# Batch 0 of a fused attention and feed-forward kernel: decay folded into V, one exponential per score block, weights loaded in thirds

## The chip, the cores and the metric

The kernel runs on one core of one Trainium2 chip. A core has five engines that each work through their own instructions in order: TensorE (PE, matrix products), VectorE (DVE), ScalarE (ACT), GpSimd (POOL) and SyncE (SP, which here only issues transfers). They wait for one another through semaphores. Transfers between the chip's memory and the core's on-chip memory (SBUF) go through 16 DMA engines, fed by queues that SP, ACT and POOL issue into. PE writes its results into PSUM, a small memory of banks of 128 x 512 float32, and the other engines copy from there.

The metric is the device time of one execution in microseconds (us); lower is better. The output has to agree with the reference within a tolerance.

## The reference

Causal attention with a decay, for 8 batches, 8 heads, 576 positions and head size 64, followed by an RMS norm and a SwiGLU feed-forward network (FFN) over the 4608 tokens:

```python
scores = scale * np.matmul(q, k.transpose(0, 1, 3, 2))       # q, k, v: (8, 8, 576, 64)
cum = np.cumsum(np.maximum(s, 0.0), axis=-1)                 # s: (8, 8, 576)
bias = -(cum[:, :, :, None] - cum[:, :, None, :])
scores = np.where(causal, -1000000000.0, scores + np.minimum(bias, 0.0))
scores = scores - np.max(scores, axis=-1, keepdims=True)
attn = np.exp(scores)
attn = attn / (np.sum(attn, axis=-1, keepdims=True) + 1e-09)
x = np.matmul(attn, v)           # heads side by side: (4608, 512)
...
rms = np.sqrt(np.mean(x * x, axis=-1, keepdims=True) + 1e-06)
xn = x / rms * rms_g
g = xn @ w_gate                  # (512, 1536)
silu = g * (1.0 / (1.0 + np.exp(-g)))
out = (silu * (xn @ w_val)) @ w_out
```

The weight of key position j for query position i is exp(score + cum[j] - cum[i]). The factor exp(-cum[i]) is the same for all keys of a query and cancels in the division by the sum, so a kernel needs only exp(score) times exp(cum[j] - shift), with one shift for each head and batch.

## The kernel before

**Tiles.** A batch has five blocks of positions (`NSC`), four of 128 and one of 64, the tail. Because of the decay, a key block kb matters only to the queries of blocks kb and kb + 1; a flag that is worked out during the run decides at the end whether this held, and a general path (`general`) stands ready otherwise. The score step `s_step(b, kb, g)` (L225) multiplies key block kb with up to 256 queries for the four heads of head group g into two PSUM banks, one for even and one for odd heads (L250). The exponentials follow on ACT, one instruction for each head (L274), because each takes its own per-partition bias, a column of `biasK` with cum[j] minus the shift. POOL then zeroes what lies above the diagonal (L283, `affine_select`). For the tail block, one step holds all eight heads.

`av_step(b, qb, g)` (L292) multiplies the exponentials of key blocks qb - 1 (L300) and qb (L306) with V. V lies in SBUF as `v_sb`, bf16, with a 65th column of ones for each head, whose product is the sum for the division. DVE takes the reciprocal (L313) and multiplies (L315) into `x_sb`. After the second head group the sum of squares is formed, on DVE (L325) or with `act=True` on ACT (L321, Square with an accumulator), and POOL makes the norm's factor from it (L328, L331). `x_scale` (L338, DVE) multiplies the block by that factor and by the norm's gain `g_row`, giving `xs_sb`. Transposed it becomes `xnT`, the FFN's input, by four PE transposes and a copy in batch 0 (`xt_step`, L357 and L364) and by a transposing DMA later.

q and k come as float32 (`kq32`), are cast to bf16 (`cast`, L139 on ACT, L141 on POOL or DVE), transposed by PE for two heads at a time (`t_step`, L184, evicted by L190 on DVE or L192 on ACT), and their tails together in `tail_step` (L200, copies L205 and L209).

**The FFN** (`ffn(c)`, L658) takes chunks of 512 tokens. Each of its 12 blocks has four gate matmuls (L668), a tanh on ACT (L671), four value matmuls (L677), and two multiplications on DVE (U at L680, `Ht` at L673 or L685). Four groups of 12 output matmuls follow (L690), with a copy (L695) and a store (L697) each. There are nine chunks, a batch being 1.125 chunks.

**Order.** From the second batch on a planner (`step`, L599) places the attention's work between the FFN's matmuls, slot by slot, from queues for each engine (`act_side`, `pool_side`, `dve_side`, `v_side`), and `need(c)` (L646) runs it further until a chunk's input is there. Batch 0's blocks 0 to 3 are written out by hand ahead of the first chunk (L773 to L884): loads, casts, transposes, scores, products, normalizations. Between them stand `warm(n)` calls (L593), dummy matmuls that keep PE busy; the loads of the FFN's weights (`load_w`, L700, GpSimd's queue, cast on the way), here in halves of the 1536 columns; and the first part of the range check (`check_mag`, `check_max`, L368 to L375), three DVE instructions that take the largest magnitude of q and k. The tail block of batch 0 (S(4), its products and x_scale) falls to the planner in the first chunk.

The PSUM banks are held by one pool `pp` for the whole run: four single banks F (FFN results; in the prologue also second score buffers through `pairF`), one double bank S, one AV and one T.

The decay (L705 to L720) starts with the load of s on ACT's DMA queue, ahead of everything on ACT. `decay_sums` takes max(s, 0), the running sum (`tensor_tensor_scan`) and subtracts the shift, four DVE instructions; `decay_bias` transposes the result by five matmuls and copies it to `biasK`.

Of the kernel before, what the change touches and what calls it, by code (L numbers as in the profile page):

```python
# [26 lines left out]
def kernel(  # L27
# [43 lines left out]
    pp = fast.enter_context(tc.tile_pool(name="pp", bufs=1, space=bass.MemoryType.PSUM))  # L71


# [26 lines left out]

    def psF():
        return pp.tile([128, DM], FP32, name="psF", tag="F", bufs=4)

    def psF16():
        return pp.tile([128, 8, 128], BF16, name="psF16", tag="F", bufs=4)

    def psS():
        return pp.tile([128, 2, 512], FP32, name="psS", tag="S", bufs=1)

    def psAV():  # L110
        return pp.tile([128, 512], FP32, name="psAV", tag="AV", bufs=1)

    def psAV16():
        return pp.tile([128, 8, 128], BF16, name="psAV16", tag="AV", bufs=1)

    def psT():
        return pp.tile([128, 8, 128], BF16, name="psT", tag="T", bufs=1)

    def psT32():
        return pp.tile([128, 512], FP32, name="psT32", tag="T", bufs=1)  # L120
# [58 lines left out]

    def t_step(b, hp, w, pT=None, dve=None):  # L180
# [44 lines left out]
    def s_step(b, kb, g, pair=None):  # L225
# [6 lines left out]
        if pair is None:  # L232
            ps = psS()
            pair = (ps[:, 0, :], ps[:, 1, :])
# [26 lines left out]
        def exps(part):  # L261
            for h, par, o in part:
# [29 lines left out]
    def av_step(b, qb, g, ps=None, act=False):  # L292
# [3 lines left out]
        for j in range(4):  # L296
            h = 4 * g + j
            o = ps[:, j * NV:(j + 1) * NV]
            if qb > 0:
                nc.tensor.matmul(o, lhsT=E[:, eslot[b, qb - 1, g], j, 128:256],  # L300
                                 rhs=v_sb[:, p, qb - 1, h, :], start=(j == 0), stop=False)
            if qb < 4:
                d = E[:, eslot[b, qb, g], j, 0:128]
            else:
                d = E[:, eslot[b, 4, 0]].rearrange("p h (a n) -> p (h a) n", n=128)[:, h, :]
# [177 lines left out]
    def after_av(b):  # L483
        if b + 2 < B:
            (early if b else later)(v_side, 6 if b else 16, [
                lambda r=r: load_v(b + 2, r) for r in range(NSC)]
                + [lambda: done.__setitem__(("V", b + 2), slot[0])])
# [16 lines left out]
    def do_s(key, pair=None):  # L504
        b, kb, g = key
        second = s_step(b, kb, g, pair)
# [193 lines left out]
    def load_w(src, dst, i):  # L700
        fs = slice(i * (DF // 2), (i + 1) * (DF // 2))
# [13 lines left out]
    def decay_bias():  # L715
# [4 lines left out]
        nc.vector.tensor_copy(out=biasK, in_=ps[:, 0:NSC * BH].rearrange("p (a e) -> p a e", e=BH))  # L720
# [50 lines left out]
    with tc.manual_schedule():  # L771

        nc.scalar.dma_start(out=s_sb, in_=s.rearrange("b h s -> (b h) s"))  # L773
# [6 lines left out]
        nc.sync.dma_start(out=g_row, in_=moe_rms_g.rearrange("(o d) -> o d", o=1).to_broadcast([128, DM]))  # L780
        make_identity(nc, ident_bf)
        make_identity(nc, ident_f)
        nc.gpsimd.memset(v_sb[:, :, :, :, 64:65], 1.0)
# [3 lines left out]
        nc.vector.memset(stat, 0.0)  # L787
        nc.vector.memset(ss_all, 0.0)
        nc.vector.memset(acc, 0.0)
        nc.vector.memset(v_sb[64:128, :, 4, :, 0:64], 0.0)  # L790
        nc.vector.memset(kqTn[:, :, :, :, 576:640], 0.0)

# [10 lines left out]
        def pairF():  # L803
            return (psF(), psF())

        def s_first(kb, g, pair=None):
            do_s((0, kb, g), pair)()

        for w in (0, 1):
            piece(w, 0, 0, ACT)  # L810
            piece(w, 0, 1, ACT)
            piece(w, 0, 2, POOL)
            piece(w, 0, 3, POOL)
        load_v(0, 0)
        load_v(0, 1)
        load_v(0, 2)
        load_w(moe_w_gate, wg_sb, 0)
# [281 lines left out]
```

## Time and profile before

| | |
|---|---|
| time, median of 3 runs | 376.12 us (375.98 to 376.18) |
| the profiled execution's own time | 375.92 us |
| its span (first to last instruction) | 374.2 us |
| first FFN matmul | 32.12 us |
| first matmul of the second chunk | 76.35 us |
| exponentials (L274) | 352 instructions, 114.9 us on ACT |
| masks (L283) | 72 instructions, 52.2 us on POOL |
| FFN matmuls (L668, L677, L690) | 432 each, 379 ns each |
| bytes moved | 46.22 MB, 124 GB/s on average |

Busy shares are of the span. The time of the run is 1.7 us longer than the span, which begins with the first recorded instruction and ends with the last. A group's line gives its count, its busy time and the mean of one, then the idle time of its engine just ahead of it and what ended most of that. "Granted clock" is the TensorE clock that the throttle allowed; it was 1.00 in the prologue and 0.998 over the span. In the timeline's lines the columns are the start in us, the duration in us, the engine, the line, the operation, what it writes and reads, the shape, and in brackets the wait just before it with what ended it; several equal instructions in a row are drawn together with "x8". In the table by stretch, the columns after the stretch are its length, then for PE, PE's weight loads, DVE, ACT and POOL the busy us and in brackets the instructions, then the granted clock, the DMA share and GB/s.

In the trace of before, s landed at 6.24 us, the first half of k and q at 6.41 and 7.64, the second at 9.12 and 10.92, their tails at 11.8 and 12.96, and `g_row` at 13.55. The first three blocks of V landed from 14.5 to 16.4, the first half of the gate weights at 19.7 and of the value weights at 25.3, the second halves at 37.2 and 41.5.

### The profile page before, as it was taken

To read this page: it belongs to the slowest core of one execution; us is meant where nothing else is said; L and a number is where in the kernel's file an instruction comes from. 1 tells how busy PE (TensorE), PEld (TensorE's weight loads), DVE (VectorE), ACT (ScalarE), POOL (GpSimd) and SP (SyncE) were. 2 spreads that over 40 slices of the span, in tenths; PEclk is the share of its full clock that TensorE was granted. 3 is DMA by queue.
4 is the path that set the end of the run, shared out by engine and by line. 5 is a ranking of instruction groups with operands and counts; after the bars stand their busy time and mean duration, and the time that the engine had idled before them with its cause. 6 is when DMAs were issued, how large, how long until landed. Compare 5 with 4: busy or idle time off the path is not lost. (4 is left out here: it accounts for less than half of the span.)

```text
span 374.2 us, 6937 instructions
## 1 busy us (share of the span) xinstructions
PE 347.0 (93%) x2356; PEld 161.4 (43%) x2356; DVE 279.7 (75%) x525; ACT 239.8 (64%) x626; POOL 174.4 (47%) x277
## 2 busy tenths in 40 slices
PE   1867899899999999899999999999999999999993
PEld 1443444454444444344444444444444444444441
DVE  6758988589887878788889897785488548837830
ACT  3777787547877597786777776777677744323321
POOL 5865734974846575779756825522322310000000
PEclk9999999999999999999999999999999999999999
DMA  8999999899997599959999997992210230020012
GB/s 230 189 227 237 146 196 220 123 204 225 155 168 105 53 195 165 159 55 204 149 162 225 136 107 152 120 67 44 96 26 14 44 105 3 0 84 31 0 44 76
DMA packets 125626, 46.22 MB, mean 124 GB/s; under 512 B 104912, under 2 KB 120784, under 8 KB 125584
## 3 DMA queue, kind: packets, MB, share of 16 engines
q0 software_dynamic: 59920, 11.80, 42.7%
q1 hardware_dynamic: 53040, 24.33, 34.6%
q10 hardware_dynamic: 12624, 9.59, 10.5%
q8 instruction: 20, 0.33, 0.4%
q14 instruction: 22, 0.18, 0.2%
HBM read 38.16 MB, written 9.44 MB: 127 GB/s over the span
## 5 line engine op out<-in xcount | busy, mean ns | idle before, releaser
L274 ACT ACTIVATE E<-psS,biasK 128x256 bf16<-128x256 f32 (+3 forms) x352 | 114.9, 415 | 19.7 <-PE psS L250 18.1
L668 PE MATMUL psF<-xnT,wg_sb 128*128 128x512 bf16 x432 | 111.1, 379 | 2.4 <-DMA xnT<-xs_sb 1.3
L677 PE MATMUL psF<-xnT,wv_sb 128*128 128x512 bf16 x432 | 111.1, 379 | 0.1
L690 PE MATMUL psF<-wout_sb,Ht 128*128 128x512 bf16 x432 | 102.3, 379 | 0.0
L283 POOL TENSOR_SCALAR_AFFINE_SELECT E<-E 128x512 bf16<-128x512 bf16 x72 | 52.2, 725 | 93.7 <-ACT E L274 92.8
L671 ACT ACTIVATE T<-psF 128x512 f32<-128x512 f32 x108 | 64.3, 597 | 42.1 <-PE psF L668 38.7
L680 DVE SCALAR_TENSOR_TENSOR U<-T,psF 128x512 bf16<-128x512 f32 x108 | 73.6, 682 | 21.9 <-ACT T L671 21.8
L673 DVE TENSOR_TENSOR Ht<-U,psF 128x512 bf16<-128x512 bf16 x99 | 67.7, 684 | 7.5 <-PE psS L250 0.5
L668 PEld LDWEIGHTS <-wg_sb 128*128 128x128 bf16 x432 | 38.7, 98 | 46.9 <-issue 8.0
L677 PEld LDWEIGHTS <-wv_sb 128*128 128x128 bf16 x432 | 38.6, 98 | 42.8 <-issue 4.6
L690 PEld LDWEIGHTS <-Ht 128*128 128x128 bf16 x432 | 38.7, 98 | 42.1 <-issue 2.3
L338 DVE SCALAR_TENSOR_TENSOR xs_sb<-x_sb,al_all,g_row 128x512 bf16<-128x512 bf16 (+1 forms) x40 | 32.8, 822 | 16.1 <-POOL al_all L331 14.5
L695 ACT ACTIVATE osb<-psF 128x512 f32<-128x512 f32 x36 | 21.4, 595 | 33.7 <-PE psF L690 29.4
L321 ACT ACTIVATE xs_sb<-x_sb 128x512 bf16<-128x512 bf16 (+1 forms) x36 | 22.9, 639 | 22.3 <-DVE x_sb L315 22.2
L175 POOL DMA_DIRECT2D v_sb<-in_v_dram x40 | 35.3, 883 | 0.4 <-issue 0.3
L375 DVE TENSOR_TENSOR acc<-acc,mag 128x1280 bf16<-128x1280 bf16 x32 | 29.4, 936 | 0.4
L250 PE MATMUL psS<-kqT 64*128 64x256 bf16 (+2 forms) x304 | 26.8, 262 | 1.6 <-ACT E L274 1.5
L306 PEld LDWEIGHTS <-E 128*128 128x128 bf16 x320 | 22.3, 99 | 13.3 <-POOL E L283 3.4
L328 POOL TENSOR_SCALAR al_all<-ss_all 128x1 f32<-128x1 f32 (+1 forms) x40 | 11.1, 277 | 28.5 <-ACT xs_sb L321 23.0
L300 PEld LDWEIGHTS <-E 128*128 128x128 bf16 x256 | 20.6, 99 | 7.9 <-DVE x_sb L315 0.6
L331 POOL TENSOR_TENSOR al_all<-al_all,mhalf 128x1 f32<-128x1 f32 (+1 forms) x40 | 22.2, 556 | 3.3
L250 PEld LDWEIGHTS <-kqT 64*128 64x128 bf16 x320 | 10.4, 97 | 29.9 <-issue 28.6
(94 smaller groups left out, 278.8 us busy)
## 6 DMA issues: line engine op xcount, KB each, us to landing
out_dram<-osb SPq DMA_DIRECT2D x36, 256.0 KB, 2.3
kq<-in_q_dram ACTq DMA_DIRECT2D x6, 1024.0 KB, 9.5
v_sb<-in_v_dram POOLq DMA_DIRECT2D x32, 128.0 KB, 7.2
kq<-in_k_dram ACTq DMA_DIRECT2D x2, 1024.0 KB, 10.6
kqn<-in_k_dram POOLq DMA_DIRECT2D x16, 128.0 KB, 5.6
wg_sb<-in_moe_w_gate_dram POOLq DMA_DIRECT2D x2, 768.0 KB, 7.3
wv_sb<-in_moe_w_val_dram POOLq DMA_DIRECT2D x2, 768.0 KB, 10.3
wout_sb<-in_moe_w_out_dram POOLq DMA_DIRECT2D x1, 1536.0 KB, 14.1
```

The source lines that it names most:

```text
L175: nc.gpsimd.dma_start(out=v_sb[0:n, b % 2, c, :, 0:64], in_=v[b, :, c * 128:c * 128 + n, :].rearrange("h p d -> p h d"))
L250: nc.tensor.matmul(pair[par][:, j * W:j * W + M], lhsT=kT, rhs=qT, start=(j == 0), stop=(j == nj - 1))
L274: nc.scalar.activation(out=eo, in_=ei, func=AF.Exp, scale=0.125, bias=biasK[:, kb, bh:bh + 1])
L283: nc.gpsimd.affine_select(out=Ev[:, :, 0:nq], in_=Ev[:, :, 0:nq], pattern=[[0, nh], [1, nq]], compare_op=ALU.is_ge, fill=0.0, base=0, chan ...
L338: nc.vector.scalar_tensor_tensor(out=xs_sb[0:n, (b * NSC + qb) % NX, :], in0=x_sb[0:n, (b * NSC + qb) % NX, :], scalar=al_all[0:n, col:col ...
L375: nc.vector.tensor_tensor(out=acc[:, sl], in0=acc[:, sl], in1=mag[:, sl], op=ALU.max)
L668: nc.tensor.matmul(Gp, lhsT=wg_sb[:, cc, fs], rhs=xnT[:, cc, x0:x0 + DM], start=(cc == 0), stop=(cc == CC - 1))
L671: nc.scalar.activation(out=T, in_=Gp, func=AF.Tanh, scale=0.5)
L673: nc.vector.tensor_tensor(out=Ht[:, fb - 1, :], in0=pend[0], in1=pend[1], op=ALU.mult)
L677: nc.tensor.matmul(Vp, lhsT=wv_sb[:, cc, fs], rhs=xnT[:, cc, x0:x0 + DM], start=(cc == 0), stop=(cc == CC - 1))
L680: nc.vector.scalar_tensor_tensor(out=U, in0=T, scalar=1.0, in1=Gp, op0=ALU.add, op1=ALU.mult)
L690: nc.tensor.matmul(Op, lhsT=Ht[:, fb, tb * 128:(tb + 1) * 128], rhs=wout_sb[:, fb, :], start=(fb == 0), stop=(fb == FB - 1))
```

## The change

It rewrites batch 0's prologue; what the planner does with the later batches stays as it is, but for two entries in the first chunk.

- **Decay in V.** For batch 0 the factor exp(cum[j] - shift) is no longer a bias of the exponentials but multiplies V's rows. ACT writes it straight into V's 65th column (one exponential of the transposed sums), so that the column's product is still the sum for the division. V of batch 0 is loaded as float32 into `v32`, which shares a buffer with `Ht`, on GpSimd's queue, and DVE multiplies it by the column (`weigh`), one instruction for each block. After batch 0 the column is set back to ones.
- **One exponential for four heads.** Without a bias, the exponentials of a score block become one instruction (128 x 1024 elements for blocks 0 to 2, 128 x 4 x 192 for block 3, 128 x 8 x 64 for the tail). It writes the heads in the order of the two banks, and `e_head` tells the products where a head lies.
- **Head.** s goes first on SP's queue, ahead of k and q. `decay_sums` is the first work of DVE after its memsets; the memsets of `stat`, `ss_all`, `acc` and of V's tail go to POOL. Third and fourth casts of the first half of q and k, and both tails' casts, go from POOL to DVE; some evictions change between ACT and DVE.
- **Order.** Two score buffers (S) from a pool of the prologue's own (`pq`: S 2, F 2, A 1, T 1), so that the next block's scores are issued ahead of the exponential of the one before; then `pp` is opened as it was before, for the FFN. All four sums of squares are on ACT (`act=True`), that of block 0 stands ahead of the exponential of S(3,1). Batch 1's q and k loads are issued earlier. The warm-up matmuls are 6 instead of 13.
- **Weights** come in thirds, the last third issued at the end of the prologue: two more DMAs on GpSimd's queue. 
- **Check.** The three check instructions for batch 0's q leave the prologue's end and are queued for the first chunk, together with the multiplication for V's tail (`weigh(DVE, 4)`, the third entry of DVE's queue).

```diff
+    v32 = mp.tile([128, NSC, H, D], FP32, name="v32", tag="Ht", bufs=2)
...
+    def load_v0(c):
+        n = rows(c)
+        nc.gpsimd.dma_start(
+            out=v32[0:n, c], in_=v[0, :, c * 128:c * 128 + n, :].rearrange("h p d -> p h d"))
+
+    def weigh(eng, c):
+        n = rows(c)
+        eng.tensor_tensor(
+            out=v_sb[0:n, 0, c, :, 0:D], in0=v32[0:n, c],
+            in1=v_sb[0:n, 0, c, :, D:NV].to_broadcast([n, H, D]), op=ALU.mult)
...
         def exps(part):
+            if b == 0:
+
+                if part[0][1] == 0 and part[0][0] == heads[0][0]:
+                    eo = Ev.rearrange("k (a j) n -> k a j n", a=2)[:, :, :, 0:N]
+                    ei = both.rearrange("k a (j n) -> k a j n", n=W)[:, :, 0:nj, 0:N]
+                    nc.scalar.activation(out=eo, in_=ei, func=AF.Exp, scale=0.125)
+                return
...
     def after_av(b):
         if b + 2 < B:
+            def ones():
+                nc.gpsimd.memset(v_sb[:, 0, :, :, D:NV], 1.0)
+                load_v(b + 2, 0)
...
     def load_w(src, dst, i):
-        fs = slice(i * (DF // 2), (i + 1) * (DF // 2))
+        fs = slice(i * (DF // 3), (i + 1) * (DF // 3))
...
-        nc.scalar.dma_start(out=s_sb, in_=s.rearrange("b h s -> (b h) s"))
+        turn = psum("pq", (2, 2, 1, 1))
+        nc.sync.dma_start(out=s_sb, in_=s.rearrange("b h s -> (b h) s"))
...
+        nc.gpsimd.memset(stat, 0.0)
+        nc.gpsimd.memset(ss_all, 0.0)
+        nc.gpsimd.memset(acc, 0.0)
...
+        decay_sums()
...
+        bias = decay_turn()
+        ACT.activation(out=v_sb[:, 0, :, :, D], in_=bias[:, :, 0:H], func=AF.Exp)
         for w in (0, 1):
+            for r in range(4):
+                piece(w, 0, r, (ACT, ACT, DVE, DVE)[r])
+        DVE.tensor_copy(out=biasK, in_=bias)
...
+        for w in (0, 1):
+            cast(DVE, 0, w, 4, 5)
+        s00 = do_s((0, 0, 0))
+        s10 = do_s((0, 1, 0))
         do_t((0, 2, 0), pT=psT(), dve=True)
         do_t((0, 3, 0), pT=psF16(), dve=True)
+        s00()
+        load_v0(3)
+        load_w(moe_w_gate, wg_sb, 0)
+        do_t((0, 2, 1), pT=psT(), dve=False)
+        do_t((0, 3, 1), pT=psF16(), dve=True)
+        s20 = do_s((0, 2, 0))
+        s10()
...
+            load_kq(nc.sync, 1, w)
...
+        s01 = do_s((0, 0, 1))
+        load_w(moe_w_val, wv_sb, 0)
+        s20()
+        s11 = do_s((0, 1, 1))
         tail_step(0)
         done["T", 0] = 0
+        s01()
+        weigh(DVE, 0)
+        weigh(DVE, 1)
+        do_av((0, 0, 0))
+        s21 = do_s((0, 2, 1))
+        s11()
+        load_v0(4)
+        do_av((0, 1, 0), psT32())
+        weigh(DVE, 2)
         s30 = do_s((0, 3, 0))
+        s21()
+        do_av((0, 0, 1), act=True)
+        s31 = do_s((0, 3, 1))
+        s30()
+        weigh(DVE, 3)
+        s31()
+        do_av((0, 2, 0), psT32())
         do_av((0, 1, 1), act=True)
+        do_av((0, 3, 0), psT32())
         x_scale(0, 0)
+        do_av((0, 2, 1), act=True)
+        do_xt((0, 0), psF16())
         warm(2)
+        x_scale(0, 1)
         do_av((0, 3, 1), psT32(), act=True)
         load_w(moe_w_gate, wg_sb, 1)
         load_w(moe_w_val, wv_sb, 1)
         do_xt((0, 1), psF16())
         warm(2)
         x_scale(0, 2)
...
         warm(2)
         x_scale(0, 3)
         do_xt((0, 3), psF16())
-        check_mag(0, 1)
-        check_max(0)
-        check_max(1)
-        done["check", 0, 1] = 0
+        load_w(moe_w_gate, wg_sb, 2)
+        load_w(moe_w_val, wv_sb, 2)
+        turn.close()
+        turn = psum("pp", (1, 4, 1, 1))
...
-        check(0, (0,))
+        check(0)
+        later(dve_side, 4, [lambda: weigh(DVE, 4)])
+        dve_side.insert(2, dve_side.pop())
```

The second argument of `psum` gives the number of buffers for the tags S, F, A and T. A call such as `s00 = do_s(...)` issues the score matmuls and the exponential; `s00()`, called later, issues the mask.

More of the change, by code (lines that the diff above doesn't have):

```diff
@@ L825 @@
[L825 to L831 removed]
+        for r in range(4):
+            piece(0, 1, r, (ACT, ACT, DVE, POOL)[r])
+        load_v0(0)
+        load_v0(1)
+        load_v0(2)
+        for r in range(4):
+            piece(1, 1, r, DVE)
+        for w in (0, 1):
+            cast(DVE, 0, w, 4, 5)
+        s00 = do_s((0, 0, 0))
+        s10 = do_s((0, 1, 0))
```

115 lines of the change are left out of this document (37 added, 78 removed).

## The prediction

> **What bounds the kernel now.** I read the engines' shares first, then the busy time by stretch, then the timeline of the first 33 us, then what TensorE (PE) waits for afterwards.
>
> ```profile
> PE 347.0 (93%) x2356; PEld 161.4 (43%) x2356; DVE 279.7 (75%) x525; ACT 239.8 (64%) x626; POOL 174.4 (47%) x277
> ```
>
> ```profile
> 10.40:20.00 9.60, 7.58 (x66) 4.79 (x65) 6.90 (x17) 7.53 (x22) 7.78 (x11) 1.00 1.80 180
> 20.00:24.00 4.00, 2.49 (x40) 1.80 (x38) 2.84 (x13) 3.62 (x12) 2.59 (x5) 1.00 1.21 194
> 24.00:28.00 4.00, 2.54 (x26) 1.22 (x25) 2.48 (x7) 2.16 (x8) 3.09 (x7) 1.00 0.96 275
> 28.00:32.10 4.10, 2.27 (x21) 1.16 (x20) 3.38 (x5) 2.91 (x6) 2.98 (x5) 1.00 1.14 294
> 32.10:76.30 44.20, 40.73 (x319) 19.58 (x319) 35.30 (x68) 30.71 (x78) 26.62 (x41) 1.00 1.14 176
> 76.30:374.20 297.90, 288.77 (x1882) 130.99 (x1878) 222.26 (x407) 188.50 (x496) 125.51 (x196) 1.00 0.81 105
> ```
>
> The busy columns are PE, weight loads, VectorE (DVE), ScalarE (ACT), GpSimd (POOL). From 32.1 us PE is bound; before that no engine is full, and batch 0's attention runs as a chain from engine to engine. Nearly all that the change edits lies there, so its worth is the shift of the first feed-forward (FFN) matmul, now at 32.12. Its last links:
>
> ```profile
> 27.77 0.42 DVE L315 TENSOR_TENSOR x_sb<-psT,rZ 128x256 bf16<-128x256 f32 x1
> 28.23 0.63 ACT L321 ACTIVATE xs_sb<-x_sb 128x512 bf16<-128x512 bf16 x1 [2.06 <-DVE x_sb L315]
> 29.65 0.55 POOL L331 TENSOR_TENSOR al_all<-al_all,mhalf 128x1 f32<-128x1 f32 x1
> 30.23 0.75 DVE L338 SCALAR_TENSOR_TENSOR xs_sb<-x_sb,al_all,g_row 128x512 bf16<-128x512 bf16 x1 [0.72 <-POOL al_all L331]
> 31.47 0.60 ACT L364 ACTIVATE xnT<-psF 128x512 bf16<-128x512 bf16 x1 [0.87 <-PE psF L357]
> 32.12 1.02 PE L668 MATMUL psF<-xnT,wg_sb 128*128 128x512 bf16 x4 [0.69 <-ACT xnT L364]
> ```
>
> From the end of the last block's normalization on DVE (28.19) to the FFN it is 3.93 us, and the change leaves these links as they are. So the question is when DVE ends that last normalization. Rows that price the path to it:
>
> ```profile
> 6.26 0.45 DVE L707 TENSOR_SCALAR s_sb<-s_sb 64x576 f32<-64x576 f32 x1 [0.76 <-DMA s_sb<-in_s_dram]
> 8.39 0.64 DVE L712 TENSOR_SCALAR shf<-cum,rng 64x576 f32<-64x576 f32 x1
> 16.36 0.68 DVE L190 COPY kqT<-psF 128x512 bf16<-128x512 bf16 x1
> 18.86 1.01 PE L200 MATMUL psT<-ident_bf,kqn 128*128 128x128 bf16 x8 [0.29 <-DVE x_sb L315]
> 20.12 0.28 DVE L209 COPY kqT<-psT 128x256 bf16<-128x256 bf16 x1
> 24.52 1.03 DVE L338 SCALAR_TENSOR_TENSOR xs_sb<-x_sb,al_all,g_row 128x512 bf16<-128x512 bf16 x1
> 28.00 0.39 PE L357 MATMUL psF<-ident_bf,xs_sb 128*128 128x128 bf16 x4
> ```
>
> After it, these waits of PE matter:
>
> ```profile
> PE psT L357 <- DVE xs_sb L338: 1.5, 1, 1.5
> PE psT L184 <- ACT kqn L139: 1.1, 1, 1.1
> ```
>
> **The change part by part.** Below, S(k,g) are the scores of key block k and head group g, AV(q,g) the products of query block q; moments are us from the span's start, laid out from the new order on each engine with durations of the rows.
>
> *Head.* The load of s goes from ACT's queue to the first place on SP's, so the k and q loads are issued one issue later (0.47 to 0.57 us) and s no longer runs beside them. Now s lands at 6.2. New landing: no later than that; no sooner than 0.92 + 2.3 = 3.2, the quickest DMA row (the output stores, 2.3 us). I take 3.5, since it is ahead of every other load. The decay sums take 2.8 (6.26 to 9.03), PE's five transposes 0.8, then comes the new exponential on ACT (128x40, 0.2 to 0.3): 7.4. ACT's four casts of k and q stand behind it; now they begin at 6.44 with k's landing. At 0.40 each they end at 9.0, the four evictions (0.60 and 0.69) at 11.1 against 10.79: **+0.3**. The four casts that POOL did are on DVE, 0.28 each, hidden behind ACT's. The memsets moved to POOL (acc, v_sb) end by about 6, ahead of its first cast at 9: nothing, as POOL idles from 2.8 to 6.47 today. Without that cover they would delay the first V loads, not the score path.
>
> *Exponentials.* 32 per-head instructions of batch 0's blocks 0 to 3 become 8. A 128x512 ACTIVATE takes 0.597 and a 128x256 cast 0.40, so 128x1024 is 0.40 + 3 x 0.197 = 1.0, against 1.57 for four; the 192-wide ones are 0.8 against 1.37. ACT loses 6 x 0.57 + 2 x 0.57 = 4.6 us of work. S(4) in the first chunk: 0.6 against 1.74.
>
> *What is late next.* DVE now casts k's and q's tails before the transposes of heads 4 to 7 are evicted. q's tail landed at 12.9, now about 13.2, so those evictions run from 13.7 instead of 12.3; the last ends at 16.3 (17.04 now). ACT: S(2,0) 16.2, S(0,1) 17.2, S(1,1) 18.2 to 19.2; now S(1,1) ends at 20.5. So here the change leads by 1.3. PE's tail transposes stand behind S(1,1), which waits for the buffer of S(2,0); their copies on DVE end at 19.3 (20.40 now).
>
> Behind those copies, in DVE's order, stand the new multiplications of V ("weigh"): 128x512 with float32 in, nearest rows 0.68 (L680) clean and 1.03 against 0.75 for L338 when POOL masks beside it. AV(0,0) waits for weigh 0, and S(2,1) stands behind AV(0,0) on PE: its exponential starts at 21.1, not 19.2. Then Square(0) stands ahead of S(3,1)'s exponential on ACT and waits for a normalization behind weigh 2; S(3,1) ends at about 25.0, as now (24.95). On POOL the 0.76 us of Square(0)'s two followers stand ahead of the masks of S(3,0) and S(3,1). The lead on ACT is spent.
>
> From 19.3 DVE has: four weighs, 0.69 to 0.9 each beside POOL's masks (I take 0.88 less an overlap of 0.08: 3.2); eight normalizations at 0.56 (L313 to the end of L315's issue): 4.5; two x_scales, 1.5; and 0.9 of waiting for the mask of S(3,0). 19.3 + 10.1 = 29.4 for the last normalization, against 28.19. Adding 3.93, and 0.2 because ACT is still at Square(2) and a copy: FFN at 33.5, **+1.4**. With clean weighs and casts it is +0.5; with s at 6.2 it is +3.8.
>
> The row behind the 0.88: POOL and DVE side by side slow each other (DVE L338 1.03 against 0.75). [...]
>
> *Weights, V and the next k, q.* POOL issues two more weight DMAs (0.75 to 0.82 each), after the last block's chain: V of batch 1 is issued about 1.6 us later in the FFN's time. Half 1 of the weights, issued 2 us ahead of the FFN, landed 7 and 10 us after issue; a third is smaller and first used at the fifth FFN block, some 10 us in: nothing. If it landed late, PE would wait there. Batch 1's k and q are loaded 7 us sooner beside the weights; nobody waits for either before 28: nothing, up to 0.5 if the first warm-up matmul waits for its weights.
>
> *First chunk (32 to 76).* Gains: the single S(4) exponential lets ACT cast sooner, where PE waits 1.1; the check's 3.4 us of DVE at the chunk's head, which held the first U from 33.8 to 34.3, goes. Loss: the same check returns later in the chunk, with weigh 4 (0.7). DVE is busy 28.9 of the 32 us from 31 to 63; 4.2 us come on the part with 3.1 idle. The chunk's end hangs on DVE and POOL (the 1.5 us wait for x_scale), so the gains inside don't reach the next chunk and some of the excess 1.1 does. Bounds -1.5 and +1.5; I take **+0.5**, half the excess. Later chunks keep their order.
>
> **Sum.** +1.4 + 0.5 = +1.9. The profiled execution took 375.92 (span 374.2); 377.8, and the median stands 0.2 above it: **378.0**.
>
> **The rivals.**
> - *The exponentials' gain arrives (faster).* If the exponentials followed one another from 16.2, S(3,1) would end at 16.2 + 4.0 + 1.6 = 21.8, 3.1 ahead of today: 373.0. It needs the weighs not to hold S(2,1); from a DVE backlog of 2 us less it decides. For: DVE idles 2.4 us before the tail copies. Against: the built order has the weighs behind them. 0.08.
> - *No net change.* Clean weighs (+0.5) and the first chunk's gains arrive by 0.5: 376.1. For: only one contended row is seen. 0.14.
> - *TensorE slow into the FFN (slower).* Transposes stand 100 ns apart at 18.86 (1.01 for eight) and 56 at 28.00: PE doubled its rate near 21, after a dense stretch. Now that stretch has a hole from 18.6 to 20.1 (weigh 0) and fewer warm-up matmuls follow (6, not 13). Eight or so links of 0.1 to 0.2 and the first FFN matmuls at double spacing: +0.9 to +1.5, 379.2. [...] Against: the tail and score matmuls from 15 to 18.6 are dense too. 0.20.
> - *s still lands near 6 (slower).* Everything on ACT waits for it: +2.4 more, 380.4. For: it shares the queues with the k and q loads that stand right behind it. 0.13.
>
> **How the numbers follow.** Forecast 0.45, rivals 0.08, 0.14, 0.20, 0.13. Within 0.2% (about what a measurement tells from no change) is 375.4 to 376.9: 0.15 with a little of the forecast's low end. Faster: 0.10, the first rival and a tail of the second. Slower: 0.75. The range of 376.0 to 380.3 leaves out the first rival and the ends of the second and last; the forecast's own range is 377.0 to 379.2.
>
> **What would show it.** Right: DVE waits for s ending near 3.5; 128x1024 exponentials near 1.0; S(2,1)'s exponential after an ACT wait of about 2 us; weighs of 0.7 to 0.9; the last normalization near 29.4 and the first FFN matmul near 33.5; the next chunk's first matmul some 2 us later than 76.35. Wrong: an FFN start before 32, s landing after 5, or a second chunk that starts no later than now.

## The result: slower by 1.1%

The changed kernel took 380.07 us (median of 4, 378.94 to 381.04) against 376.05 us (median of 4, 375.22 to 376.18) on the same chip: a ratio of 1.0111, 95% interval 1.0076 to 1.0145. That is 4.0 us more, within the range given (376.0 to 380.3), and about twice the shift of +1.9 that was forecast. The profiled execution is the longest of the four, 381.04 us with a span of 379.5.

| moment, us from the span's start | before | forecast | after |
|---|---|---|---|
| s lands | 6.24 | 3.5 | 3.6 |
| exponential of S(2,1) starts | 20.89 | 21.1 | 21.85 |
| exponential of S(3,1) ends | 24.95 | 25.0 | 26.2 |
| last normalization ends | 28.2 | 29.4 | 31.6 |
| first FFN matmul | 32.12 | 33.5 | 35.21 |
| first matmul of the second chunk | 76.35 | 78.3 | 80.59 |
| end of the span | 374.2 | | 379.5 |

So 3.1 us are lost before the FFN and 1.2 us in its first chunk. Of the remaining 1.0, 0.4 lie in chunks two to four and 0.6 in the last chunk. From its first matmul to the end of the span the last chunk takes 37.2 to 37.9 us in the profiles of all kernels below, whatever was changed, so those 0.6 are no property of the change.

First the engines' shares, then busy time by stretch (same columns as before):

```profile
PE 347.2 (91%) x2305; PEld 162.7 (43%) x2349; DVE 280.1 (74%) x529; ACT 235.1 (62%) x598; POOL 174.9 (46%) x279
```

```profile
20.00:24.00 4.00, 2.84 (x29) 1.44 (x29) 3.52 (x7) 1.80 (x2) 1.59 (x3) 1.00 1.15 280
24.00:28.00 4.00, 2.32 (x31) 1.79 (x30) 2.55 (x10) 2.14 (x5) 2.17 (x6) 1.00 1.14 285
28.00:32.10 4.10, 2.92 (x21) 1.72 (x20) 3.25 (x8) 1.66 (x4) 1.26 (x3) 1.00 0.55 155
```

ACT has lost work as promised (239.8 us to 235.1). From 20 to 24 DVE is nearly full, as forecast; from 24 to 32 it is not, and that is where the forecast went wrong. The timeline shows what the chain hangs on:

```profile
19.83 1.61 DVE L198 TENSOR_TENSOR v_sb<-v,v_sb 128x512 bf16<-128x512 f32 x2
20.89 0.38 PE L340 MATMUL psAV<-v_sb,E 128*128 128x65 bf16 x4 [1.50 <-DVE v_sb L198]
21.85 1.80 ACT L294 ACTIVATE E<-psS 128x1024 bf16<-128x1024 f32 x2 [2.26 <-PE psS L277]
22.96 1.16 DVE L198 TENSOR_TENSOR v_sb<-v,v_sb 128x512 bf16<-128x512 f32 x1
24.77 0.63 ACT L355 ACTIVATE xs_sb<-x_sb 128x512 bf16<-128x512 bf16 x1 [1.12 <-DVE x_sb L349]
25.85 0.57 POOL L365 TENSOR_TENSOR al_all<-al_all,mhalf 128x1 f32<-128x1 f32 x1
26.39 1.21 POOL L317 TENSOR_SCALAR_AFFINE_SELECT E<-E 128x512 bf16<-128x512 bf16 x2
27.68 0.18 DVE L347 RECIPROCAL rZ<-psT 128x4 f32<-128x4 f32 x1 [1.31 <-PE psT L340]
30.97 0.18 DVE L347 RECIPROCAL rZ<-psT 128x4 f32<-128x4 f32 x1 [0.78 <-PE psT L340]
32.33 0.48 PE L391 MATMUL psF<-ident_bf,xs_sb 128*128 128x128 bf16 x4
```

V's multiplications (L198) hold AV(0,0) and S(2,1) as forecast: ACT waits 2.26 us. But then DVE itself waits, 1.31 us for AV(3,0), which needs the mask of S(3,0). POOL makes that mask at 26.39 although the exponential was done at 23.65, since block 0's norm factor (L365) stands ahead of it. And 0.78 us for AV(3,1), which stands behind the first transposes of x on PE. The last line is a group of four transposes that takes 0.48 us; those at 30.75 still took 0.61, those at 34.12 took 0.40. PE doubles its rate only here, near 32.5 us, against 21 us before.

At the end of the first chunk there is something that the profile of before does not have. The rows are stretches cut where the granted clock changes, then a line of PE's waits, then the eight output matmuls behind the wait, in the kernel before and in the changed one:

```profile
32.54:76.92 44.38, 39.72 (x308) 19.21 (x313) 35.09 (x69) 30.80 (x74) 28.80 (x45) 1.00 1.15 176
76.92:80.33 3.41, 3.41 (x12) 1.20 (x10) 0.42 (x1) 0.00 (x0) 3.40 (x6) 0.50 0.96 157
```

```profile
PE psT L391 <- DVE xs_sb L372: 2.6, 1, 2.6
```

```profile
74.39 1.89 PE L690 MATMUL psF<-wout_sb,Ht 128*128 128x512 bf16 x8
76.94 3.57 PE L727 MATMUL psF<-wout_sb,Ht 128*128 128x512 bf16 x8
```

PE waits 2.6 us for the last x_scale (1.5 before), and behind that wait the granted clock is at 0.50 for 3.41 us: the eight output matmuls there take 3.57 us instead of 1.89. In the table of stretches the column reads 1.00 also ahead of the first change on record (21.07 us before, 32.54 after); there the spacing of the matmuls tells the rate.

### The profile page after: what moved, and what is told of

It reads as the page before. It is cut to its first block, busy times and chain, and to the rows that moved or that the text cites. A ratio compares the mean times of both kernels' runs of the same rounds, so it can differ in the third digit from the quotient of the medians.

```text
span 379.5 us, 6853 instructions
## 1 busy us (share of the span) xinstructions
PE 347.2 (91%) x2305; PEld 162.7 (43%) x2349; DVE 280.1 (74%) x529; ACT 235.1 (62%) x598; POOL 174.9 (46%) x279
## 5 line engine op out<-in xcount | busy, mean ns | idle before, releaser
L308 ACT ACTIVATE E<-psS,biasK 128x256 bf16<-128x256 f32 (+3 forms) x328 | 107.0, 413 | 19.6 <-PE psS L277 18.1
L714 PE MATMUL psF<-xnT,wv_sb 128*128 128x512 bf16 x409 | 109.2, 380 | 1.3
L277 PE MATMUL psS<-kqT 64*128 64x256 bf16 (+2 forms) x320 | 28.9, 268 | 2.6 <-ACT E L308 1.0
L186 POOL DMA_DIRECT2D v_sb<-in_v_dram x35 | 30.5, 873 | 0.7 <-POOL v_sb L520 0.3
L409 DVE TENSOR_TENSOR acc<-acc,mag 128x1280 bf16<-128x1280 bf16 x32 | 28.6, 907 | 0.3
L340 PEld LDWEIGHTS <-E 128*128 128x128 bf16 x320 | 23.1, 101 | 13.4 <-issue 2.5
L362 POOL TENSOR_SCALAR al_all<-ss_all 128x1 f32<-128x1 f32 (+1 forms) x40 | 11.9, 297 | 35.5 <-ACT xs_sb L355 28.6
L334 PEld LDWEIGHTS <-E 128*128 128x128 bf16 x256 | 21.1, 101 | 9.4 <-issue 1.8
L365 POOL TENSOR_TENSOR al_all<-al_all,mhalf 128x1 f32<-128x1 f32 (+1 forms) x40 | 22.2, 556 | 3.3
```

The costliest lines, as they stand in the source:

```text
L186: nc.gpsimd.dma_start(out=v_sb[0:n, b % 2, c, :, 0:64], in_=v[b, :, c * 128:c * 128 + n, :].rearrange("h p d -> p h d"))
L277: nc.tensor.matmul(pair[par][:, j * W:j * W + M], lhsT=kT, rhs=qT, start=(j == 0), stop=(j == nj - 1))
L308: nc.scalar.activation(out=eo, in_=ei, func=AF.Exp, scale=0.125, bias=biasK[:, kb, bh:bh + 1])
L409: nc.vector.tensor_tensor(out=acc[:, sl], in0=acc[:, sl], in1=mag[:, sl], op=ALU.max)
L714: nc.tensor.matmul(Vp, lhsT=wv_sb[:, cc, fs], rhs=xnT[:, cc, x0:x0 + DM], start=(cc == 0), stop=(cc == CC - 1))
```

## The experiments

Each kernel is the changed one with the edit shown; each was compared with the kernel before on the same chip. The kernels ran on several chips, where the kernel before took 375.42 to 376.05 us, so the ratios compare better than the medians. "FFN start" is from the one profiled execution, and can move by some 0.4 us without a cause in the edit: "check back", whose edit lies behind all that is in question here, starts 0.37 sooner because V's block 2 got ahead of a mask of POOL and took 0.68 us instead of 1.16.

| kernel | FFN start | median us (range) | ratio to before, 95% interval |
|---|---|---|---|
| the changed kernel | 35.21 | 380.07 (378.94 to 381.04) | 1.0111 (1.0076 to 1.0145) |
| V's multiplications earlier | 33.57 | 378.11 (377.19 to 379.00) | 1.0056 (1.0039 to 1.0072) |
| prologue holes filled | 34.81 | 378.25 (376.07 to 381.56) | 1.0083 (1.0040 to 1.0126) |
| wait in the chunk filled | 35.27 | 380.13 (378.75 to 380.89) | 1.0103 (1.0071 to 1.0135) |
| masks ahead of the norm | 34.61 | 380.43 (377.86 to 381.89) | 1.0100 (1.0054 to 1.0146) |
| tails' casts later | 34.70 | 379.08 (378.47 to 381.80) | 1.0074 (1.0052 to 1.0096) |
| check back | 34.84 | 378.49 (378.10 to 380.11) | 1.0078 (1.0051 to 1.0105) |
| weights in halves | 35.27 | 379.94 (378.50 to 382.33) | 1.0104 (1.0072 to 1.0137) |
| four changes of order | 33.38 | 377.40 (376.11 to 381.38) | 1.0050 (1.0023 to 1.0077) |
| the same, memset moved | 31.69 | 375.49 (374.25 to 378.48) | 1.0014 (0.9988 to 1.0040) |
| all waits filled | 33.66 | 377.18 (375.53 to 379.86) | 1.0059 (1.0032 to 1.0086) |
| without V's multiplications | 32.75 | 377.92 (376.28 to 379.95) | 1.0052 (1.0024 to 1.0081) |
| order, memset and fills | 31.24 | 374.08 (373.68 to 375.23) | 0.9958 (0.9943 to 0.9973) |

**V's multiplications earlier.**

```diff
+        for c in range(3):
+            weigh(DVE, c)
         tail_step(0)
...
-        weigh(DVE, 0)
-        weigh(DVE, 1)
         do_av((0, 0, 0))
...
-        weigh(DVE, 2)
```

> One edit to the changed kernel: the multiplications of V's blocks 0, 1 and 2 stand ahead of the copies of the transposed tails on DVE, where DVE idles from 16.9 to 19.4 us; the copies come at 19.4 as now. Theory V-queue (the prediction's: the multiplications behind the tail copies hold AV(0,0), and all that stands behind it on PE, ACT and POOL): AV(0,0) starts near 19.3 instead of 20.9, the exponential of S(2,1) near 20.1 instead of 21.85, S(3,1)'s ends near 23.8 instead of 26.2, and the first FFN matmul moves from 35.2 to 32.5-33.0; the time falls by 2.2 to 2.7 us. Theory PE-rate (PE stays at half rate until 32 us because its work has holes): PE, without the hole from 19.2 to 20.9, doubles its rate near 21 to 24 and the FFN starts still earlier, 31.5-32.3. Theory POOL-order (the norm's factor of block 0 ahead of the masks holds the end): at most 0.8 us gained, FFN near 34.4.

```profile
18.31 1.73 DVE L198 TENSOR_TENSOR v_sb<-v,v_sb 128x512 bf16<-128x512 f32 x2
21.07 1.80 ACT L294 ACTIVATE E<-psS 128x1024 bf16<-128x1024 f32 x2 [0.60 <-PE psS L277]
```

The FFN starts at 33.57, later than expected. In this execution the second half of q landed later (12.56 us against 11.11), so that the transposes of its heads 4 to 7 began at 16.03 us instead of 15.14. By the clock the FFN is 1.6 us earlier; counted from that moment, 2.5, which is what the theory V-queue says. ACT's wait ahead of S(2,1) shrank from 2.26 to 0.60. POOL-order alone is out (FFN was to stay near 34.4). PE-rate got no support: the clock rose at 31.8, as late as ever.

**Prologue holes filled.** Five dummy matmuls ahead of the transposes of q's heads 4 to 7, three ahead of AV(0,0). `warmk(n)` is `warm(n)` with transposed keys as the operand, since the weights have not landed yet:

```diff
+        warmk(5)
         do_t((0, 2, 1), pT=psT(), dve=False)
...
+        warmk(3)
         do_av((0, 0, 0))
```

> The changed kernel with eight dummy matmuls on already transposed keys in PE's two holes, five from 12.7 to 15.1 us and three from 19.2 to 20.9; nothing else is moved. Theory PE-rate: PE doubles its rate by 21 us (128-column transposes 56 ns apart instead of 107 at the first FFN transposes) and the links of PE behind it shorten: FFN near 34.0 instead of 35.2, time 1.0 to 1.4 us less. Theory V-queue or POOL-order (the order sets the end, PE's rate is a matter of tenths): PE doubles its rate, too, but the FFN starts no earlier than 34.8; time down by 0.4 at most.

```profile
16.49:23.32 6.83, 5.27 (x61) 2.87 (x60) 4.33 (x12) 5.24 (x6) 4.93 (x8) 1.00 0.92 151
23.32:33.56 10.24, 7.17 (x57) 4.06 (x56) 6.90 (x18) 5.16 (x13) 4.86 (x11) 0.50 1.13 262
```

The rate doubled at 16.5 us and fell again at 23.3, until 33.6, with the later holes. The FFN started 0.4 us sooner, no more than it can move by itself. So this run did not test what a steady fast PE is worth; it shows that an early rise does not last by itself.

**Wait in the chunk filled.**

```diff
+        if key == (1, 3):
+            warm(8)
         xt_step(b, qb, pX)
```

> The changed kernel with eight dummy matmuls (1.7 us) ahead of the transposes of batch 1's fourth block, in the wait of 2.64 us for x_scale at the end of the first chunk, behind which the granted clock falls to 0.50 for 3.8 us in the profiled run. Theory clock-gap (a wait of PE that long makes the clock fall, the 1.5 us of before does not): the clock stays at 1.00 there, the eight output matmuls behind the wait take 1.9 us instead of 3.6, the second chunk starts 1.7 us sooner (44 us behind the first instead of 45.4), and the times lie at or below the quickest run of the changed kernel (378.9), 378.3 to 379.0. Rival (the clock falls for another reason, such as the load of the chip): the fall stays in the profile, times spread as before, 378.9 to 381.

```profile
35.66:39.07 3.41, 3.41 (x9) 1.22 (x8) 1.24 (x2) 1.63 (x3) 3.00 (x4) 0.50 1.19 193
```

The fall behind the wait is gone: the wait is 0.5 us, and the part of the chunk from the first output matmul on takes 14.9 us instead of 17.0. But this execution had a fall of 3.41 us at the FFN's start instead, and the median is unchanged. The theory was right about the place and wrong about the sum. (The fall in the changed kernel's profile lasted 3.41 us, not the 3.8 put above.)

**Masks ahead of the norm.**

```diff
-        do_av((0, 0, 1), act=True)
+        do_av((0, 0, 1), act="later")    # without Square and its two followers
...
         s31()
+        square(0, 0, True)
```

> The changed kernel with the sum of squares of block 0 (ACT) and its two followers (POOL) behind the exponential and the masks of S(3,0) and S(3,1) instead of ahead of them. Theory POOL-order: the mask of S(3,0) comes near 23.8 instead of 26.4, AV(3,0) near 25.9 instead of 27.1, the FFN near 34.1 instead of 35.2; time down by 0.9 to 1.2 us. Theory V-queue (DVE is full from 19.4 to the last normalization): DVE only idles elsewhere, FFN within 0.3 of 35.2, time the same.

```profile
23.01 2.26 POOL L317 TENSOR_SCALAR_AFFINE_SELECT E<-E 128x512 bf16<-128x512 bf16 x3 [1.99 <-ACT E L294]
24.65 1.16 DVE L198 TENSOR_TENSOR v_sb<-v,v_sb 128x512 bf16<-128x512 f32 x1
```

The masks come one after another at 23.0, and AV(3,0)'s normalization at 27.1 instead of 27.7. The gain at the FFN is 0.6 us, half of what was expected: the multiplication of V's block 3 now runs beside a mask and takes 1.16 us instead of 0.69, and AV(3,1) still waits on PE. Its times lie 4 us apart. The profiled execution, the longest at 381.89 us, has two falls of 3.41 us, at 34.65 and at 79.03; the shortest, 377.86 us, has a mean clock of 0.998, which leaves room for none.

**Tails' casts later.**

```diff
-        for w in (0, 1):
-            cast(DVE, 0, w, 4, 5)
         s00 = do_s((0, 0, 0))
...
+        s20 = do_s((0, 2, 0))
         do_t((0, 2, 1), pT=psT(), dve=False)
         do_t((0, 3, 1), pT=psF16(), dve=True)
-        s20 = do_s((0, 2, 0))
+        for w in (0, 1):
+            cast(DVE, 0, w, 4, 5)
```

> The changed kernel with the two casts of the tails on DVE behind the copies of the transposed keys and queries of heads 4 to 7 instead of ahead of them, and the score matmuls of S(2,0) ahead of the last two groups of transposes. Theory V-queue/head (the tail casts hold the second head group, and all behind it): the transposes of q's heads 4 to 7 start near 14.0 us instead of 15.1, the exponential of S(1,1) ends near 18.2 instead of 19.6, AV(0,0) starts near 19.7 instead of 20.9, and the FFN near 34.0 instead of 35.2; time down by about 1.2 us. Rival (the landings of q and V set these moments, or what stands behind absorbs it): AV(0,0) at 20.5 or later, FFN at 34.8 or later, time down by 0.4 at most.

S(1,1) ended at 19.45, not at 18.2, and the FFN started at 34.70; neither theory holds as put. What held the first head group is seen on DVE: max(s, 0) took 2.56 us, and S(0,0)'s exponential came at 13.36 instead of 11.51, late enough to use up what the later casts had freed. That led to the memset below. In this execution the clock rose only at 37.4 us, so the first chunk began at half rate.

**Check back.** One part of the change undone:

```diff
+        check_mag(0, 1)
+        check_max(0)
+        check_max(1)
+        done["check", 0, 1] = 0
         turn.close()
...
-        check(0)
+        check(0, (0,))
```

> The changed kernel with one part undone: the three check instructions of batch 0's q are at the end of the prologue again, not in the first chunk. Theory (the check's move shortened the first chunk's gate and value part by 1.7 us, yet not the work that the last x_scale of the chunk waits for, so that the wait of PE grew from 1.5 to 2.6 us and the clock falls behind it): the gate and value part takes near 30 us instead of 28.4, the wait is near 1.2, no fall of the clock behind it, the second chunk starts 44 to 44.5 us behind the first instead of 45.4; times 378.5 to 379.3, so 0.5 to 1.5 below the median of the changed kernel. Rival (the move is a plain gain, the fall has to do with other things): the second chunk starts later, time 0.5 to 1.5 longer than that of the changed kernel.

The gate and value part took 28.6 us, not 30: the 1.7 us that the changed kernel gains there (28.4 against 30.1 before) do not come from the check. The wait for the last x_scale was 2.1 us, not 1.2, and there was no fall in this profile. With the check moved, the wait was 2.2 to 2.7 us where nothing was put into it, and the first chunks without a fall took 43.7 to 43.9 us against 43.4 here. So no gain of the check's move is seen; that it lengthens the wait is not shown either.

**Weights in halves.** Another part undone: `load_w` cuts at half the columns, and the last two loads fall away.

> The changed kernel with one part undone: the weights in halves again, two DMAs fewer on POOL's queue at the end of the prologue. Prediction's step (costed at nothing): FFN start, first chunk and time as with thirds, within 0.4 us and the spread of the clock's falls (378.9 to 381). Rival (POOL's 1.5 us of issuing hold the casts and V loads behind them, and with these the chunk's last x_scale): the wait for x_scale falls from 2.6 to near 1.2 us and the time by 1 us or more.

Within the spread, as the prediction's step has it: FFN start 35.27, wait 2.3 us, median 0.13 us below the changed kernel's.

**Four changes of order**: the three above that move V's multiplications, the norm of block 0 and the tails' casts, and this one:

```diff
         do_av((0, 2, 1), act=True)
+        do_av((0, 3, 1), psT32(), act=True)
         do_xt((0, 0), psF16())
         warm(2)
         x_scale(0, 1)
-        do_av((0, 3, 1), psT32(), act=True)
```

> The changed kernel with four changes of order together: V's first three multiplications ahead of the tails' copies on DVE, the tails' casts behind the copies of heads 4 to 7 and S(2,0)'s scores earlier, the sum of squares of block 0 behind the masks of S(3,0) and S(3,1), and the last products AV(3,1) ahead of the first transposes of x on PE. Theory order (the gain of the merged exponentials is there and is lost in the order behind): the exponential of S(3,1) ends near 21.7 us instead of 26.2, the last normalization near 25.7 instead of 31.6, the FFN starts at 29.3 to 30.5, ahead of the 32.1 of before; time 374 to 375.5 with the clock's falls, 373.2 where there are none. Rival (some engine is simply full, DVE above all): the FFN starts at 32 or later, time 376.5 or more.

33.38 us: better than any of the three that were tried alone, and 3 to 4 us short of the expectation. Two things were in the way. max(s, 0) took 2.59 us again, and with the later steps tightened this was now on the path; and the first multiplication of V took 1.68 us beside three masks of POOL.

**The same, memset moved.**

```diff
-        nc.gpsimd.memset(acc, 0.0)
...
         do_xt((0, 3), psF16())
+        nc.vector.memset(acc, 0.0)
```

> The four changes of order together, and with them one part of the change undone in another place: the memset of acc goes from POOL's start to DVE's end of the prologue. In most profiles the first decay instruction on DVE, max(s, 0), took 2.6 us instead of 0.47 and ended when that memset of POOL (2.5 us) ended. Theory lock (a DVE instruction of that kind and POOL's memset exclude each other; which comes first is a matter of some 0.05 us): max(s, 0) takes 0.47 us, the column's exponential comes near 7.6 instead of 9.45 us, S(0,0)'s near 11.5 instead of 13.35, the FFN starts at 31.7 to 32.5 instead of 33.4, and the time falls by 1 to 1.7 us against the four changes alone. Rival (the instruction is slow for its own reason, such as s landing in parts): it still takes 2.6 us, and nothing moves. Second rival (q's landing near 12.5 and the V multiplications beside POOL's masks absorb it): max(s, 0) is quick, the FFN starts at 33 or later.

In three kernels, DVE's max(s, 0) and the POOL instructions beside it: the changed one, the one with the wait in the chunk filled, and this one.

```profile
3.65 0.47 DVE L744 TENSOR_SCALAR s_sb<-s_sb 64x576 f32<-64x576 f32 x1 [0.83 <-DMA s_sb<-in_s_dram]
3.75 0.41 POOL L824 MEMSET stat<- 128x4 f32 x1
3.85 2.49 POOL L826 MEMSET acc<- 128x2560 bf16 x1
```

```profile
3.74 2.65 DVE L746 TENSOR_SCALAR s_sb<-s_sb 64x576 f32<-64x576 f32 x1 [0.93 <-DMA s_sb<-in_s_dram]
3.75 0.10 POOL L826 MEMSET stat<- 128x4 f32 x1
3.85 2.23 POOL L828 MEMSET acc<- 128x2560 bf16 x1
```

```profile
3.85 0.45 DVE L749 TENSOR_SCALAR s_sb<-s_sb 64x576 f32<-64x576 f32 x1 [1.04 <-DMA s_sb<-in_s_dram]
```

In the first DVE began at 3.65 and POOL's memset of four columns took 0.41 us, until DVE was done. In the second DVE began 0.09 us later, POOL's memset took 0.10, and DVE ended only when the memset of `acc` had ended (6.1 to 6.4 us). Without that memset the instruction takes 0.45 us. Of the eleven profiles with the memset on POOL's start, nine show 2.52 to 2.68 us and two 0.47 and 0.50. The lock theory holds, and its gain arrives here: FFN at 31.69, 1.7 us sooner, and the time 1.4 us less than that of the four changes alone when each is set against the kernel before on its chip. The second rival falls.

**All waits filled**, the order of the changed kernel untouched: the eight dummies in the prologue, `warm(4)` ahead of AV(3,0), `warm(3)` ahead of the first transposes of x, and the eight in the chunk.

> The changed kernel, order untouched, with dummy matmuls in PE's waits: five from 12.7 us, three ahead of AV(0,0), four ahead of AV(3,0), three ahead of the first transposes of x, eight ahead of the last transposes in the first chunk. [...] Rival (the falls come from load or chance): falls remain and the spread stays near 2 us.

The clock rose at 15.8 us and did not fall in the profiled execution as long as PE had work; the FFN started at 33.66, 1.55 us sooner than in the changed kernel with the same order. That is what the late rise costs. But the executions still lie 4.3 us apart. Whether falls went on in the others is not shown. Their mean clocks (0.988 to 0.999) do not tell, since the profiled one has 0.994 with no fall in its work: the last 4.35 us of its span, where PE had finished, stand at 0.50.

**Without V's multiplications.**

```diff
-        ACT.activation(out=v_sb[:, 0, :, :, D], in_=bias[:, :, 0:H], func=AF.Exp)
+        ACT.activation(out=v_sb[:, 0, :, :, D], in_=bias[:, :, 0:H], func=AF.Exp, scale=0.0)
...
-        load_v0(0)
+        load_v(0, 0)
...
-        weigh(DVE, 0)
```

> The changed kernel without the decay: the column of V is all ones and the five multiplications of V are left out (V comes cast, by the same queue), so what is measured is the changed order without its new work on DVE. In the changed kernel's profile the four of the prologue are 3.46 us of DVE. Theory V-queue (they stand on the path by their place and length): AV(0,0) starts near 19.4 us instead of 20.9, the last normalization near 28.5 to 29 instead of 31.6, the FFN near 32.3 to 33 instead of 35.2; time 2.2 to 3 us less than that of the changed kernel, 376.5 to 378. Rival (POOL's order and the late transposes hold the end whatever DVE does): FFN at 34 or later, time 1.2 us less at most.

The other four multiplications go too, and with scale 0 the column is all ones, so batch 0 goes without the decay. AV(0,0) at 19.24, the FFN at 32.75: with their place and length the multiplications cost 2.5 us of the 3.1. Without the whole of this new work the changed order still starts the FFN 0.6 us later than before, so the gain of the exponentials is lost to other things too.

**Order, memset and fills.** The version before last, with dummies at six places:

```diff
+        warmk(4)                         # ahead of the transposes of q's heads 4 to 7
+        warmk(3)                         # ahead of AV(1,0)
+        warm(2)                          # ahead of AV(3,0)
+        warm(2)                          # ahead of the first transposes of x
+        warm(4)                          # behind them, instead of 2
+            warm(8)                      # ahead of the last transposes in the first chunk
```

> The four changes of order and the memset's move, and dummy matmuls in PE's waits: four ahead of the transposes of q's heads 4 to 7, three ahead of AV(1,0), two ahead of AV(3,0), two ahead of and two more behind the first transposes of x, eight ahead of the last transposes of the first chunk. Theory clock: the clock rises by 17 us instead of 31.5, the FFN starts at 30.2 to 31 instead of 31.7, falls are rarer; median 373.5 to 374.7, below the 375.4 to 376 of the kernel before. Rival (the clock's grid makes falls and late rises in most executions all the same, or dummies delay what follows): median 375 or more.

```profile
14.77 0.39 PE L206 MATMUL psT<-ident_bf,kqn 128*128 128x128 bf16 x4
31.24 1.02 PE L717 MATMUL psF<-xnT,wg_sb 128*128 128x512 bf16 x4 [0.69 <-ACT xnT L403]
```

Four transposes take 0.39 us from 14.8 on (0.59 at 15.14 in the changed kernel). The FFN starts only 0.45 us sooner than without the dummies, a little later than expected, but the executions lie within 1.6 us of each other (six) instead of 4.2 (ten), and 374.08 us is below the 375.82 of the kernel before on that chip: ratio 0.9958, 0.9943 to 0.9973.

## Why the prediction was right or wrong

**Head.** s landed at 3.6 as taken, and the first exponentials came at 11.5. "The memsets moved to POOL: nothing, as POOL idles" was wrong as a step: POOL idles, but beside its memset of `acc` max(s, 0) took up to 2.68 us instead of 0.47. In the changed order that cost nothing at the FFN's start: it began at 35.21 with max(s, 0) at 0.47 us and at 35.27 with 2.65. In the first execution DVE came to the casts of q's second half and the tails 1.9 us sooner, but they went slowly beside POOL's issue of V's loads (0.51 us each, 0.25 where POOL was idle), and ended at 14.49 against 14.55. So the rival "s lands near 6" had its effect on the chain's head in nine of eleven profiles, by another cause, and its price (+2.4) was wrong: what stood behind took it up.

**Exponentials.** Two of 128x1024 in a row took 1.94 us, against 1.0 each worked out. S(1,1) ended at 19.6 (19.2 forecast): right but for DVE's casts, taken at 0.28 us each. Those seven took 3.55 us in the changed kernel's profile, and 1.76 in the execution that had them later, when POOL was idle.

**What is late next.** The chain through V's multiplications was forecast link by link and came so: S(2,1) at 21.85 (21.1), S(3,1) ending at 26.2 (25.0). The four multiplications took 3.46 us (3.2 taken): two paid for POOL's work beside them (1.01 and 1.16 us), two did not (0.68 and 0.69). With more masks beside it one went to 1.68. That all four would pay alike, 0.88 us each, was the author's estimate, and no run shows it.

**The step that failed** is "from 19.3 DVE has ..., plus 0.9 of waiting: 29.4 for the last normalization". It took DVE for full but for that 0.9. Behind the tails' copies it waited 2.5 us for PE, 0.41, 1.31 and 0.78: the second for POOL's mask behind block 0's norm factor, the third for AV(3,1) behind the first transposes of x. So the waiting was 1.6 us more than taken: the mask's wait was seen and put too low, and AV(3,1)'s, which stood in the listing of the new order, was not seen. Another 0.6 us is that DVE's copies ended at 19.92 and not at 19.3. The last normalization was 2.2 us late in all; the links behind it then took 3.6 us and not the 4.1 put down (3.93 and 0.2). Of the two orders the experiments show one by itself, 0.6 us for the masks; AV(3,1) was moved only together with the rest, and all four changes of order and the memset give 3.5 us.

That the time lies inside the stated range is partly luck. The forecast's own range, 377.0 to 379.2, misses it, and the range's upper end was drawn for the rival with s near 6, which did not happen.

**PE's rate** was a rival (0.20, +0.9 to +1.5) and should have been in the sum: PE doubled its rate at 32.5 us, and with the same order and PE's waits filled the FFN started 1.55 us sooner. In the traces every stretch at 1.00 or 0.50 that is closed on both sides lasts a multiple of 3.41 us (3.41, 6.83, 10.24, 44.38 us). A wait of 2.64 us was followed by a fall here, and so were waits of 2.2 and 2.3 in the kernels with later casts and with halves.

**First chunk.** +0.5 was taken, +1.2 measured in the profiled execution, as a sum of other terms: the gate and value part 1.7 shorter, the wait for x_scale 1.1 longer, and 1.7 of lost clock behind it. The gain in the gate and value part is the one that was forecast. In the kernel before PE waits there 1.1 us for a cast that stands on ACT behind the exponentials of S(4); in the changed kernel those are one instruction, and the wait is gone:

```profile
35.92 1.74 ACT L274 ACTIVATE E<-psS,biasK 128x64 bf16<-128x64 f32 x8
39.01 0.59 ACT L294 ACTIVATE E<-psS 128x512 bf16<-128x512 f32 x1
```

That the gains inside would not reach the next chunk was wrong: the six profiles without a fall in the first chunk have it at 43.4 to 43.9 us, against 44.2 before. That a longer wait of PE can also halve its rate for 3.4 us was not seen; without that the first chunk would be 0.5 us shorter than before. So the sign of the +0.5 came right by a cause that was not in it. Two of the four executions of the changed kernel have a mean clock of 0.997 (378.94 and 379.58 us), which leaves no room for a fall of 3.41 us, half a percent of the clock; two have 0.993 and 0.994 (381.04 and 380.57), and the profile of the first of these shows one. So near 3 of the 4 us are the FFN's start, and the rest is how often the clock falls. The second statement is argued from these means and one profile, not shown for each execution: a low mean alone does not prove a fall, as the kernel before has an execution with 0.982 at 375.42 us beside one with 0.997 at 375.44.

**Weights in thirds, earlier loads of k and q** at nothing: right for the thirds; the loads were not tried by themselves. That the single exponential of S(4) shortens the gate and value part is read from the traces and was not tried by itself; the check does not.

## What to carry to other kernels

Merging instructions on one engine pays only where the next link can move up: of the 4.6 us that ACT saved nothing came out at the FFN as the kernel was built, and 0.4 us (31.69 against 32.12) once V's multiplications, masks, norm and transposes were put in the order in which their inputs arrive and the memset was moved. Follow each engine's queue to the end of the chain, and look at what the engine that seems full waits for. Count a hole in PE's work twice in a prologue, once for its length and once for the rate behind it (1.55 us of the FFN's start here), and before putting work on an idle POOL look at what DVE does at that moment (here 0.47 us became 2.65).

## What was not expected of the hardware

DVE's max(s, 0) and POOL's memsets held each other up: beside the memset of `acc` max(s, 0) took 0.47 and 0.50 us in two profiles, where the memset of `stat` took 0.41 instead of 0.10, and 2.52 to 2.68 in nine; without it, 0.45. It was quick in the two profiles where s landed at 3.60 and 3.62 us, and slow in the nine where s landed at 3.68 or later. The running sum, an instruction of another kind, took 1.35 us beside the same memset and 1.35 behind it. Which of the two is held up the recorded starts do not tell: in "masks ahead of the norm" DVE's record begins at 3.71 us, 0.14 ahead of that of the memset, and max(s, 0) took 2.68. Casts and multiplications on DVE paid as well: casts 0.25 us alone and 0.51 beside POOL's issue of loads, V's multiplication 0.68 alone, 1.16 beside one mask and 1.68 beside three. Where the multiplication kept its 0.68 us beside a mask, the mask could be the one to pay (in "the same, memset moved" two masks took 1.77 us instead of 1.21).

Whether a wait of PE lowers its clock is not decided by its length alone: waits of 2.2, 2.3, 2.6 and 2.7 us were followed by a fall, others of 2.1, 2.3 and 2.7 were not. Nor is it decided by PE's busy share alone. Counted in steps of 3.41 us from the recorded changes, the clock fell behind steps in which PE was busy for 0.23 (the changed kernel, 73.50 to 76.92 us, with the whole wait of 2.64 us in it), 0.49 ("masks ahead of the norm", up to 34.65), 0.53 ("wait in the chunk filled", 32.25 to 35.66) and 0.70 of the time ("prologue holes filled", up to 23.32), and did not fall behind one with 0.45 ("four changes of order", 73.24 to 76.65). No run varied this by itself, so what sets the clock is not shown.
